# Retention of the later segments: from one chunk of one sequence a step to one chunk of two sequences a step, with the upper quarter of the scores left out

## The chip, the cores and the metric

The kernel runs on one core of one Trainium2 chip. The metric is the device time of one execution in microseconds. The kernel before takes 714.7 us, the median of three runs from 714.23 to 714.72; the profiled execution spans 715.2 us. All data are float32.

## The reference

Two blocks stand one after the other. The first is a recurrent retention over 4 sequences, 8 heads, 768 positions and head size 64:

```
for t in range(S):
    state = gamma * state + outer(k[t], v[t])      # per sequence and head, 64 x 64
    y[t]  = scale * q[t] @ state
```

Its output, 3072 rows of 512, is the input `x` of a feed-forward block with 1536 hidden units:

```
g   = x @ w_gate
out = (g * sigmoid(g) * (x @ w_val)) @ w_out
```

The recurrence is computed by chunks of 128 positions. Inside a chunk, `y[t]` is a sum over `s <= t` of `(q[t] . k[s]) * gamma^(t-s)` times `v[s]` ("scores", a decay mask, "mixing"), plus `q[t]`, decayed, times the state before the chunk ("old state"). Then the state is decayed and `k^T v` of the chunk is added, with `k` decayed ("new state"). Of the 128 by 128 scores of a head only those with `s <= t` count: for the upper half of `s` (64 to 127) and the lower half of `t` (0 to 63) all are zero.

## The kernel before

**Segments.** The rows are worked off in four segments. A segment is three chunks of two sequences, so 6 chunks and 768 rows. For the first segment the retention comes first. After that the program goes round a loop with `s` from 0 to 3: an up projection with gate (`up` for the first segment, `up2` for the later ones), then a down projection (`down`). The matrix products are a fast scheme with seven products in place of eight, in `up2` applied twice over, so there are many sums of blocks (`sums_x` and `sums_2` for the inputs, `sums_u` for the weights, `sum_h` for the hidden units), which VectorE (DVE) computes.

**Retention between the products.** The retention of segment `s + 1` is done inside the down projection of segment `s`. `down` calls `step()` after each of its products; there are 21 such calls in a segment. `retention` (line 468) makes a list of closures, and the tables `DUE` (line 858; the first for `s` = 0, the second for the others) say at which of the 21 calls the next closure is emitted. The order on each engine is the order in which the program emits; nothing is rearranged by a scheduler.

**One step.** `chunk(n)` emits, in this order: `scores` of the next chunk (line 389 on TensorE, the mask product of line 395 on DVE into `midp`), `mix` of this chunk (old state, line 453; mixing, line 456; four copies to `xT` on ScalarE, line 465), `decay` (four ScalarE copies of the state with a factor), `state` (line 429, and a DVE sum, line 434), the loads of the chunk after next, and, on GpSimd (POOL), the products that put the decays on `q` and `k` of the next chunk (lines 403 and 408). Scores go through banks 4 and 5, mixing through 6 and 7, the new state through 3.

**Shapes on TensorE.** A head has 64 columns, so the products use parts of the 128 by 128 array. Scores and old state are products of 64 rows and 64 columns of weights, and the loops are ordered so that neighbours use the four quarters in turn. Mixing and new state have 128 rows and 64 columns, and neighbours use the two column halves in turn. The products of `up2` (line 643) and `down` (lines 726 and 735) use the whole array.

**Weights.** During the down projection of `s` = 0 DVE computes sums of weight blocks (lines 171, 175, 179) which are loaded from DRAM and stored back (`load_unit`, `sums_u`); later up projections load the sums. Input loads and weight loads are issued by SyncE in the order of the program; results are stored from ScalarE's queue (line 803). Places for `q`, `k`, `v` of chunks are the buffer `loadp` and two of the six weight buffers of `ring`, which also serve `up2`; each reuse waits for the last reader.

**The end.** The last unit of `down` copies its last product (`T4`) to SBUF with one ScalarE instruction (line 797) and stores two blocks of 128 rows by 512 columns.

The core of the loop order in `scores` before:

```
for n in range(NP):
    for m in (slice(0, D), slice(D, P)):      # halves of s
        for i in range(2):                    # head of the pair
            r = ds(D * i, D)
            nc.tensor.matmul(sp[i][m, ts(n, P)], kt[r, n, m], qt[r, n], ...)
```

Of the kernel before, what the change touches and what calls it, by code (L numbers as in the profile page):

```python
# [16 lines left out]
P = 128  # L17
# [7 lines left out]
L = 3  # L25
# [8 lines left out]
RING = 6  # L34

# [6 lines left out]
def tile_retnet_swiglu(  # L42
# [46 lines left out]
    def place(name, n):  # L89
# [3 lines left out]
        ("hsp", 4 * FH * P), ("midp", 4 * 512), ("loadp", 8 * 512), ("iop", 6 * 512)))  # L93
# [21 lines left out]

    def places_of(n):


        if n % 3 == 2:
            return [ring[4 + i // 2][:, ts(i % 2, 512)] for i in range(4)]  # L120
        return [loadp[:, ts(4 * (n % 3) + i, 512)] for i in range(4)]
# [244 lines left out]
    states = [consts.tile([P, NP, D], F32, name=f"state{i}") for i in range(4)]  # L366
    xT = consts.tile([P, NC, 2, TH], F32, name="xT")
    xsa = consts.tile([P, 4, KH, TH], F32, name="xs")
    xs = [xsa[:, i] for i in range(4)]

# [7 lines left out]
    def state_of(c, old=0):  # L378
        return states[2 * (c // NCK % 2) + (c + old) % 2]

    def scores(c):
        kt, qt = (pairs(t) for t in chunks[c][:2])
        sp = [bank("s") for i in range(2)]

        for n in range(NP):
            for m in (slice(None),) if c in first_chunks else (slice(0, D), slice(D, P)):
                for i in range(2):
                    r = ds(D * i, D)
                    nc.tensor.matmul(sp[i][m, ts(n, P)], kt[r, n, m], qt[r, n],  # L389
                                     start=(n == 0), stop=True, skip_group_check=True)  # L390
        a = []
        for i in range(2):
            j = turn["a"] = turn.get("a", -1) + 1
            t = pairs((iop if c in first_chunks else midp)[:, ts(j % 4, 512)])
            nc.vector.tensor_tensor(t, pairs(sp[i]), mask[:, i], op=ALU.mult)
            a.append(t)
        att[c] = a
# [38 lines left out]
    def mix(c):  # L436

        ci, seq, pos = c % NCK, c // NCK % 2, ts(c % L, P)  # L440
        qd, vn = pairs(chunks[c][1]), chunks[c][2]
        a = att.pop(c)
        prev = state_of(c, 1)
        if c in first_chunks:
            y = [pairs(banks[(0, 1, 2, 3, 7, 6)[first_chunks.index(c)]])]
            own = [(n, i, i, y[0][:, n]) for n in range(NP) for i in range(2)]
        else:
            y = [bank("y")[:, : 2 * P].rearrange("p (b t) -> p b t", b=2) for i in range(2)]
            own = [(2 * h + b, i, h, y[i][:, b])
                   for b in range(2) for i in range(2) for h in range(2)]  # L450
        for k, (n, i, h, to) in enumerate(own if ci else []):
            r = ds(D * i, D)
            nc.tensor.matmul(to[ds(D * h, D)], prev[r, n], qd[r, n],  # L453
                             start=k < 2 * len(y), stop=False, skip_group_check=True)
        for k, (n, i, h, to) in enumerate(own):
            nc.tensor.matmul(to[ds(D * h, D)], vn[:, ts(2 * n + i, D)], a[i][:, n],  # L456
                             start=(ci == 0 and k < 2 * len(y)), stop=True,
                             skip_group_check=True)
        if c in first_chunks:
            att[c] = y[0]  # L460
            nc.scalar.copy(xT[:, :, seq, pos], att[c])
        else:
            for h in range(2):
                for i in range(2):
                    nc.scalar.copy(xT[ds(D * i, D), ds(2 * h, 2), seq, pos],  # L465
                                   y[i][ds(D * h, D)])

    def retention(s):

        cs = seg_chunks(s)

        def chunk(n):
            if n + 1 < len(cs):
                scores(cs[n + 1])
            if n >= 0:
                mix(cs[n])
                decay(cs[n])  # L480
                state(cs[n])
                del chunks[cs[n]]
                if n + 3 < len(cs):
                    load_chunk(cs[n + 3], places_of(n))
            if n + 1 < len(cs):
                scale_k(cs[n + 1])
                scale_q(cs[n + 1])

        steps = []
        for n in range(-1, len(cs)):  # L490
            steps.append(lambda n=n: chunk(n))
            if n == 5:
                steps.append(lambda: sums_2(1, 2))
            if n > 0 and n % 2:
                steps.append(lambda n=n: sums_x(n // 2))
        return steps
# [222 lines left out]
    def down(s, u, step):  # L719
# [4 lines left out]
        def product(o, slot, a, start=True):  # L724
            for k in range(FH):
                nc.tensor.matmul(o, a[:, k], wot[k][:, slot], start=(start and k == 0),  # L726
                                 stop=(k == FH - 1), skip_group_check=True)
# [14 lines left out]
        def second(u):  # L742
            z = banks[2][:, :DH]
            product(z, B21, a_dn(0, 1, u))
            to = iop[:, ts(2 * (u % 2), DM)]
            tt(to[:, :DH], z, first_dn.pop(u), op=ALU.add)
            step()

# [40 lines left out]
        tt(ev[1][:, DH:], x, p5, op=ALU.add)  # L789
        more(3)  # L790
# [5 lines left out]
        product(x, T4, a_dn(1, 1, u), start=False)  # L796
        nc.scalar.copy(ev[1][:, :DH], x)  # L797
        p, pos = divmod(s * L, NCK)

        def store():  # L800
            for i in range(2):
                row = (2 * p + i) * S + (pos + u) * P
                nc.scalar.dma_start(out=out[ds(row, P)], in_=ev[i])

        if u < L - 1 or s == NSEG - 1:
            store()
        step()
        return store


    kept_vk = consts.tile([P, 2, 512], F32, name="kept_vk")

    def warm_up(n):

        for _ in range(n):
# [4 lines left out]
    warm = consts.tile([P, P + 1], F32, name="warm")  # L820
# [37 lines left out]
    DUE = [(5, 7, 9, 10, 11, 13, 14, 15, 17, 18, 19, 20),  # L858
           (3, 5, 7, 8, 9, 11, 12, 13, 15, 16, 18, 20)]
# [20 lines left out]
    for s in range(NSEG):  # L880
        nxt = seg_chunks(s + 1) if s + 1 < NSEG else []
        if s == 0:
            for i in range(3):
                load_chunk(nxt[i], places_of(i))
        else:

            ends = [(7 * n + 13.4, lambda i=i: load_chunk(nxt[i], places_of(i)))
                    for i, n in ((0, NU - 5), (2, NU - 4), (1, NU - 3)) if nxt]
# [9 lines left out]
            ends.append((5, store))  # L898
            up2(s, prepared, ends)
# [5 lines left out]
        if nxt:  # L905
            att.clear()
            steps = retention(s + 1) + [lambda: sums_2(5, 6)]
        count, sums = [0, 0, 0], []

        def step():  # L910

            k = count[0] = count[0] + 1
            if not nxt:
                return
            if s:
                if k in DUE[1]:
# [4 lines left out]
            if count[1] < len(to_sum) + 1 and k > 1 and count[1] < 3 + count[2] // 3:  # L921
# [5 lines left out]
            if k in DUE[0]:  # L927
                steps.pop(0)()
            while sums and count[2] * 12.5 < (k - 6) * 3 * len(to_sum):
                sums.pop(0)()  # L930
                count[2] += 1

        for u in range(L):
            store = down(s, u, step)
        for st in sums:
            st()
        if nxt:
            sums_2(7)
            sums_2(3)
            sums_2(4)  # L940
# [49 lines left out]
```

## Time and profile before

| | |
|---|---|
| time, median of 3 | 714.7 us |
| span of the profile | 715.2 us |
| TensorE busy | 699.7 us, 98% |
| VectorE busy | 467.5 us, 65% |
| ScalarE busy | 257.7 us, 36% |
| GpSimd busy | 239.3 us, 33% |
| DMA | 139.09 MB, mean 194 GB/s |

The stages follow each other in time. The first retention and the first up projection end at about 153 us. The down projections that hold the later retentions lie at about 155 to 219, 319 to 388 and 489 to 555 us, the up projections with `up2` between them, and the last down projection, which holds no retention, begins at about 658 us.

How to read the rows: each row of groups has the line, the engine, the operation, the tensors, `rows*columns` of the weights (for TensorE), the shape, the number of records, the busy time and the mean time of one in ns, then the idle time before them and what ended it. TensorE rows have two records for each float32 matmul of the program. A row of the timeline begins with its start and its length in us; `x` is the number of records in it.

### The profile page before, as it was taken

To read this page: it belongs to the slowest core of one execution; us is meant where nothing else is said; L and a number is where in the kernel's file an instruction comes from. 1 tells how busy PE (TensorE), PEld (TensorE's weight loads), DVE (VectorE), ACT (ScalarE), POOL (GpSimd) and SP (SyncE) were. 2 spreads that over 40 slices of the span, in tenths; PEclk is the share of its full clock that TensorE was granted. 3 is DMA by queue.
4 is the path that set the end of the run, shared out by engine and by line. 5 is a ranking of instruction groups with operands and counts; after the bars stand their busy time and mean duration, and the time that the engine had idled before them with its cause. 6 is when DMAs were issued, how large, how long until landed. Compare 5 with 4: busy or idle time off the path is not lost.

```text
span 715.2 us, 12349 instructions
## 1 busy us (share of the span) xinstructions
PE 699.7 (98%) x4832; PEld 608.7 (85%) x4832; DVE 467.5 (65%) x836; ACT 257.7 (36%) x538; POOL 239.3 (33%) x147
## 2 busy tenths in 40 slices
PE   6998999999999999999999999999999999999997
PEld 6754555578889999998888999998888999999886
DVE  3787998777769887876264575757652656657420
ACT  2658777512322332431332333332332233243000
POOL 0423444504100728380220355373210072735000
PEclk9999999999999999999999999999999999999999
DMA  9698888714999958652633556560473265630010
GB/s 325 222 359 284 284 282 268 269 47 119 405 346 356 343 191 294 206 207 79 220 145 104 175 201 198 199 207 17 120 279 133 82 207 202 201 113 1 16 43 30
DMA packets 60826, 139.09 MB, mean 194 GB/s; under 512 B 4576, under 2 KB 27616, under 8 KB 60768
## 3 DMA queue, kind: packets, MB, share of 16 engines
q1 hardware_dynamic: 57312, 132.01, 53.7%
q10 hardware_dynamic: 3456, 6.29, 2.4%
q8 instruction: 38, 0.62, 0.4%
q14 instruction: 20, 0.16, 0.1%
HBM read 101.72 MB, written 36.57 MB: 193 GB/s over the span
## 4 chain that ended last, share of the span: by engine, by line
PE 68%; DVE 1%; issue 0%; ACT 0%; DVEq 0%
PE bank L643 40%; PE bank L726 20%; PE bank L735 3%; PE bank L389 2%; PE bank L456 2%; PE bank L453 1%; PE bank L429 1%; DVE iop L608 0%; DVE ring L171 0%; DVE loadp L598 0%; DVE loadp L600 0%; DVE loadp L597 0%; ACT hsp L608 0%; DVE ring L179 0%; ACT iop L797 0%
## 5 line engine op out<-in xcount | busy, mean ns | idle before, releaser
L643 PE MATMUL bank<-loadp,ring 128*128 128x192 f32 x720 | 140.2, 327 | 0.0
L726 PE MATMUL bank<-wot,hsp 128*128 128x256 f32 x576 | 129.8, 382 | 0.0
L726 PEld LDWEIGHTS bank<-wot,hsp 128*128 128x128 f32 x576 | 108.0, 190 | 15.9 <-issue 1.0
L643 PEld LDWEIGHTS bank<-loadp,ring 128*128 128x128 f32 x720 | 120.5, 190 | 1.0 <-ACT midp L608 0.7
L608 DVE TENSOR_TENSOR iop<-bank,iop 128x384 f32<-128x384 f32 x144 | 79.7, 556 | 54.8 <-PE bank L643 51.1
L643 PE MATMUL bank<-xs,ring 128*128 128x192 f32 x432 | 87.8, 326 | 0.0
L608 ACT COPY hsp<-bank 128x384 f32<-128x384 f32 x90 | 43.0, 479 | 100.4 <-PE bank L643 90.8
L678 POOL TENSOR_TENSOR hT<-iop 128x768 f32<-128x768 f32 x36 | 67.1, 1865 | 34.8 <-DVE iop L608 34.8
L643 PEld LDWEIGHTS bank<-xs,ring 128*128 128x128 f32 x432 | 73.1, 190 | 0.0
L608 POOL TENSOR_TENSOR iop<-hsp,midp 128x768 f32<-128x768 f32 x9 | 16.3, 1813 | 163.4 <-ACT hsp L608 135.1
L643 PE MATMUL bank<-xT,ring 128*128 128x192 f32 x324 | 66.3, 327 | 1.1 <-DVE iop L608 1.1
L532 PE MATMUL bank<-xs,ring 128*128 128x384 f32 x192 | 64.7, 488 | 1.7 <-ACT iop L558 0.8
L726 PE MATMUL bank<-wot,hT 128*128 128x256 f32 x288 | 65.7, 381 | 0.1
L726 PEld LDWEIGHTS bank<-wot,hT 128*128 128x128 f32 x288 | 54.2, 190 | 8.1 <-DVE iop L789 0.5
L532 PEld LDWEIGHTS bank<-xs,ring 128*128 128x128 f32 x192 | 36.1, 190 | 28.5 <-ACT iop L558 1.7
L643 PE MATMUL bank<-hsp,ring 128*128 128x192 f32 x288 | 56.7, 326 | 0.5 <-ACT hsp L608 0.5
L643 PEld LDWEIGHTS bank<-xT,ring 128*128 128x128 f32 x324 | 54.7, 190 | 2.5 <-DVE iop L608 2.2
L532 PE MATMUL bank<-xT,ring 128*128 128x384 f32 x144 | 49.6, 489 | 1.7 <-DVE hT L569 1.6
L465 ACT COPY xT<-bank 64x256 f32<-64x256 f32 x72 | 26.5, 368 | 68.3 <-PE bank L456 67.5
L643 PEld LDWEIGHTS bank<-hsp,ring 128*128 128x128 f32 x288 | 48.4, 190 | 0.8 <-ACT hsp L608 0.8
L608 DVE TENSOR_TENSOR midp<-bank,midp 128x384 f32<-128x384 f32 x72 | 39.9, 555 | 13.8 <-PE bank L643 12.4
L532 PEld LDWEIGHTS bank<-xT,ring 128*128 128x128 f32 x144 | 27.0, 190 | 21.5 <-DVE hT L569 2.2
(147 smaller groups left out, 955.6 us busy)
## 6 DMA issues: line engine op xcount, KB each, us to landing
ring<-unitt SPq DMA_DIRECT2D x50, 896.0 KB, 4.7
unitt<-ring SPq DMA_DIRECT2D x21, 896.0 KB, 5.6
unitb<-ring SPq DMA_DIRECT2D x12, 896.0 KB, 6.9
ring<-unitb SPq DMA_DIRECT2D x21, 512.0 KB, 6.0
out_dram<-iop ACTq DMA_DIRECT2D x24, 256.0 KB, 2.8
loadp<-in_w_val_dram SPq DMA_DIRECT2D x18, 256.0 KB, 3.9
loadp<-in_w_gate_dram SPq DMA_DIRECT2D x9, 512.0 KB, 6.9
midp<-in_w_out_dram SPq DMA_DIRECT2D x12, 256.0 KB, 6.4
```

What stands on the lines that cost most here:

```text
L389: nc.tensor.matmul(sp[i][m, ts(n, P)], kt[r, n, m], qt[r, n], start=(n == 0), stop=True, skip_group_check=True)
L429: nc.tensor.matmul(st[ds(D * i, D), n], kd[:, h], vn[:, h], start=(n == 0), stop=True, skip_group_check=True)
L453: nc.tensor.matmul(to[ds(D * h, D)], prev[r, n], qd[r, n], start=k < 2 * len(y), stop=False, skip_group_check=True)
L456: nc.tensor.matmul(to[ds(D * h, D)], vn[:, ts(2 * n + i, D)], a[i][:, n], start=(ci == 0 and k < 2 * len(y)), stop=True, skip_group_check= ...
L465: nc.scalar.copy(xT[ds(D * i, D), ds(2 * h, 2), seq, pos], y[i][ds(D * h, D)])
L532: nc.tensor.matmul(o, w[:, slot, k], a[:, k], start=(start and k == 0), stop=(stop and k == KH - 1), skip_group_check=True)
L608: events.append((t, len(events), lambda: fn(*args, **kw)))
L643: nc.tensor.matmul(o[:, h], w[:, h, slot], rhs, start=(start and h == 0), stop=True, skip_group_check=True)
L678: by_block(9.5, 13.5, lambda r: pool(to[:, r], u2[:, r], p5[:, r], op=add))
L726: nc.tensor.matmul(o, a[:, k], wot[k][:, slot], start=(start and k == 0), stop=(k == FH - 1), skip_group_check=True)
L735: nc.tensor.matmul(o, a_dn(0, 0, u)[:, k], wot[k][:, B11], start=(k == 0), stop=(k == FH - 1), skip_group_check=True)
```

## The change

**Pairs.** A step of the later segments is now one chunk of both sequences (a "pair"), so a segment has three pairs. States of the two sequences lie side by side in one tile, and their decay, their new state and its sum are done for both together.

**Scores by parts.** `scores_of(p, g)` does half of the heads (`g`) of a pair: for the lower half of `s` all 128 columns of `t`, for the upper half of `s` the upper 64 columns of `t` alone. The quarter of the scores which the mask sets to zero is not computed. Results and masks of a group are 384 columns wide in place of 512. The lower `s` of sequence 0 and of sequence 1 go to different halves of the partitions. So that the mixing finds scores and `v` on the same partitions, the halves of the second sequence's `v` and `k` are loaded changed over, and new tables (`load_side`, `kdec_b`) hold mask and decay in the same layout.

**Mixing by parts.** The mixing is `low` (lower `s`, all `t`) and `high` (upper `s`, upper `t`), both with 64 rows and 64 columns of weights. `old` runs in two halves.

**Order.** `begin(p)` emits half of the old states, `low`, the first group of scores of the next pair, and the new state; `end(p)` the second group, `high`, the other old states, eight copies to `xT`, the masks of the second group, the loads for pair 2 and the POOL products, which are held in `later` and emitted two at a step. `both` is `begin` and `end` in one step. `DUE` is new, and the weight sums follow a table `SUMS`.

**Aside from the retention.** The sums `sums_2(7)`, `(3)` and `(4)`, which stood at the end of the down projection, are emitted among the first stages of `up2`. In the last unit of the last segment the results are stored in parts as they are ready, and the last product is done in two halves of 128 columns.

The diff, cut to its core:

```diff
-            for m in (slice(None),) if c in first_chunks else (slice(0, D), slice(D, P)):
-                for i in range(2):
-                    r = ds(D * i, D)
-                    nc.tensor.matmul(sp[i][m, ts(n, P)], kt[r, n, m], qt[r, n],
-                                     start=(n == 0), stop=True, skip_group_check=True)
...
-        def chunk(n):
-            if n + 1 < len(cs):
-                scores(cs[n + 1])
-            if n >= 0:
-                mix(cs[n])
-                decay(cs[n])
-                state(cs[n])
-                del chunks[cs[n]]
-                if n + 3 < len(cs):
-                    load_chunk(cs[n + 3], places_of(n))
-            if n + 1 < len(cs):
-                scale_k(cs[n + 1])
-                scale_q(cs[n + 1])
...
+        def scores_of(p, g):
+
+            kt, qt = ([pairs(t) for t in given[p][w]] for w in range(2))
+            for b in range(2):
+                for m in range(2):
+                    for r in range(2):
+                        x, n = half[r], 2 * g + b
+                        mm(banks[4 + r][half[m], ts(b, P)], kt[m][x, n, half[0]],
+                           qt[m][x, n], b == 0)
+            for b in range(2):
+                for m in range(2):
+                    for r in range(2):
+                        x, n = half[r], 2 * g + b
+                        mm(banks[4 + r][half[m], ds(2 * P + D * b, D)],
+                           kt[1 - m][x, n, half[1]], qt[1 - m][x, n, half[1]])
+
+            def decayed():
+                for i in range(2):
+                    j = turn["b"] = (turn.get("b", -1) + 1) % 6
+                    att[p, g, i] = midp[:, ts(j, TA)]
+                    nc.vector.tensor_tensor(att[p, g, i], banks[4 + i][:, :TA],
+                                            side[g][:, i], op=ALU.mult)
...
+        def low(p, first):
+            for i in range(2):
+                for b in range(2):
+                    for h in range(2):
+                        for r in range(2):
+                            n = 2 * h + b
+                            mm(y_of(n, i, r), given[p][2][r][half[r], ts(2 * n + i, D)],
+                               att[p, h, i][half[r], ts(b, P)], first and i == b == 0)
+
+        def high(p):
             for h in range(2):
                 for i in range(2):
+                    for b in range(2):
+                        for r in range(2):
+                            n = 2 * h + b
+                            mm(y_of(n, i, 1 - r, half[1]),
+                               given[p][2][1 - r][half[r], ts(2 * n + i, D)],
+                               att[p, h, i][half[r], ds(2 * P + D * b, D)])
...
+        def begin(p):
+            ci = cs[2 * p] % NCK
+            while later:
+                later.pop(0)()
+            if ci:
+                old(p, False)
+            low(p, ci == 0)
+            if p + 1 < L:
+                scores_of(p + 1, 0)
+            state_from(p)
+
+        def end(p):
+            if p + 1 < L:
+                after = scores_of(p + 1, 1)
+            high(p)
+            if cs[2 * p] % NCK:
+                old(p, True)
+            for c in range(2):
+                for h in range(2):
+                    for i in range(2):
+                        nc.scalar.copy(xT[half[i], ds(2 * h, 2), c, ts(p, P)],
+                                       y_both(h, i, c))
+            if p + 1 < L:
+                after()
+            if p == 0:
+                load_pair(s, 2, (0, 1, 2, 3))
+            if p + 1 < L:
+                scale(p + 1)
...
+        return [lambda: scores_of(0, 0), second, lambda: both(0), lambda: sums_x(0),
+                lambda: both(1), lambda: sums_x(1), lambda: begin(2), lambda: end(2),
+                lambda: sums_2(1, 2), lambda: sums_x(2), lambda: sums_2(5, 6)]
...
-        product(x, T4, a_dn(1, 1, u), start=False)
-        nc.scalar.copy(ev[1][:, :DH], x)
...
+        for c in (ts(0, DH // 2), ts(1, DH // 2)) if last(u) else (ds(0, DH),):
+            product(x, T4, a_dn(1, 1, u), start=False, cols=c)
+            nc.scalar.copy(ev[1][:, c], x[:, c])
+            if last(u):
+                store(1, ev[1], c)
...
-    DUE = [(5, 7, 9, 10, 11, 13, 14, 15, 17, 18, 19, 20),
-           (3, 5, 7, 8, 9, 11, 12, 13, 15, 16, 18, 20)]
+    DUE = [(5, 7, 9, 10, 14, 15, 16, 19, 19, 20, 21), (2, 4, 7, 8, 10, 12, 15, 18, 19, 20, 21)]
+
+    SUMS = (0, 0, 0, 0, 0, 0, 0, 2, 3, 1, 3, 3, 2, 3, 1, 2, 3, 3, 3, 2, 2)
...
+            ends += [(t, lambda p=p: sums_2(p)) for t, p in ((8, 7), (15, 3), (22, 4))]
...
-        if nxt:
-            sums_2(7)
-            sums_2(3)
-            sums_2(4)
```

## The prediction

> **What bounds the kernel now.** I read the page first, then the TensorE rows group by group, then the waits, then short stretches of the timeline.
>
> ```profile
> PE 699.7 (98%) x4832; PEld 608.7 (85%) x4832; DVE 467.5 (65%) x836; ACT 257.7 (36%) x538; POOL 239.3 (33%) x147
> ...
> PEclk9999999999999999999999999999999999999999
> ```
>
> TensorE is busy for 98% of the span at full clock, so the kernel is as long as its matmuls. In the table by stretches it is busy for 57.86 of the 58.00 us of the first later segment (160.5 to 218.5), 62.00 of 62.00 in the second and 63.00 of 63.00 in the third. The waits agree: after the first 160 us only a few tenths remain. So what a change to the retention is worth is TensorE time, read from its own rows (lines 389 scores, 453 old state, 456 mixing, 429 new state):
>
> ```profile
> L389 PE MATMUL bank<-loadp 64*64 64x128 f32 x384 | 13.2, 275 | 0.0
> L456 PE MATMUL bank<-midp,loadp 128*64 128x128 f32 x192 | 13.1, 279 | 0.0
> L429 PE MATMUL bank<-loadp 128*64 128x64 f32 x160 | 6.3, 222 | 0.0
> L453 PE MATMUL bank<-loadp,state 64*64 64x128 f32 x160 | 6.2, 269 | 0.0
> ```
>
> The mean of one (275 ns) is latency; these matmuls overlap. The trace has two records for each matmul of the program (384 + 192 records of line 389 on loadp and ring for 18 chunks of 16). One step of the middle of a segment shows their true rate:
>
> ```profile
> 167.00 0.38 PE L726 MATMUL bank<-wot,hsp 128*128 128x256 f32 x1
> 167.31 1.10 PE L389 MATMUL bank<-loadp 64*64 64x128 f32 x32
> 168.24 0.62 PE L453 MATMUL bank<-loadp,state 64*64 64x128 f32 x16
> 168.78 1.09 PE L456 MATMUL bank<-midp,loadp 128*64 128x128 f32 x16
> 169.71 0.63 PE L429 MATMUL bank<-loadp 128*64 128x64 f32 x16
> 170.27 0.48 PE L726 MATMUL bank<-wot,hT 128*128 128x256 f32 x1
> ```
>
> Inside these groups the single starts come in "waves". With 64*64 blocks of the array, four records start within 20 ns, and the next four 109 ns later; with 128*64 blocks two start together, every 109 ns for 128 columns and every 58 ns for 64 columns. So a wave costs 109 or 58 ns by its columns, whether two or four blocks work in it. This chunk is 8 + 4 + 8 waves of 109 and 8 of 58 ns: 2.64 us. From the last product of the down projection to the next took 3.27 us in starts, of which 0.22 is that product's own pitch, and the first product after it lost 0.10 us more: 3.15 us. The other 0.5 us are three changes of block shape, 0.17 us each.
>
> [...] four blocks side by side, and 0.17 us a change. [...] line 682 takes 0.95 us alone and 1.81 us at 316.69 beside line 408.
>
> **Part 1, scores (before line 389, after line 502).** A pair of chunks had 2 x 8 = 16 waves of 109 ns. Now, for each of two halves g, 8 matmuls of 128 columns (lower s, all t) and 8 of 64 columns (upper s, upper t), both rotating over four blocks: 2 x (4 x 109 + 4 x 58) = 1.34 us instead of 1.74. That four blocks can keep up at 58 ns is not in a row; but after each change of shape the second set of four weight loads starts 55 ns after the first set (167.309, then 167.364), so I take 58; 109 is the other end.
>
> **Part 2, mixing.** It had 16 waves of 109 ns a pair, 1.74 us. Now `low` (16 matmuls of 128 columns, rows h and r innermost, so four blocks) is 8 waves of 109 ns, 0.87 us; `high` (16 of 64 columns) has h outermost, so neighbours alternate between the two row halves of one column half. In program order that is two blocks a wave: 16 waves of 58 ns, 0.93 us. Together 1.80 us: nothing gained. If the blocks of the other h could start early it would be 8 waves, 0.46 us less a pair; that is the other end.
>
> **Part 3, old and new state.** 8 waves of 109 and 16 of 58 ns a pair, as before. The decay copies and the sum go over both sequences in one instruction: ACT and DVE, which have the room (16 to 17 of 58 to 63 us, and 29 to 43).
>
> **Part 4, waves and changes by segment.** First and third segment (chunks 3 to 5: old state always, new state for two pairs). Before: 0.87 + 4 x 2.64 + 2.18 + 1.31 = 14.94 us and 20 changes, 18.3 us; the starts give 18.37. After: two steps of scores 0.67 each, two of `both` with 0.44 + 0.87 + 0.67 + 0.93 + 0.67 + 0.93 + 0.44 = 4.94, `begin` 1.31, `end` 1.36: 13.88 us, and 2 + 2 + 4 + 4 + 2 + 2 = 16 changes, 2.7 us: 16.6. Saved 1.8. Second segment (chunks 0 to 2): before 14.99 and 20 changes, 18.4; after 13.94 and 17, 16.8. Saved 1.6. All three: **5.1 us**, all on the path.
>
> **Part 5, new waits.** `both` runs two groups of scores through banks 4 and 5, so the second must wait for the two DVE products of the first. Queued behind it on TensorE are `high`, the old states and the next down product. Between the two groups stands the new state, 0.93 us and two changes, 1.2 us; DVE needs about 0.22 for the last matmul's end and 1.02 for two products of 384 columns (row L608, 128x384, 556 ns alone, 1.01 for two in line). That leaves about 0.05 us for each of six: +0.3. If DVE is behind by one sum (0.68 to 0.95 us) each costs up to 0.9, +5 in all. The q products on POOL (1.28 to 1.96 us each) must be done when `begin` starts: two steps of 2.6 us after the scores, so they are hidden.
>
> **Part 6, loads and sums moved.** Pair loads replace chunk loads of the same bytes; the tables added are about 0.8 MB, in a stretch (150 to 162 us) where the DMA queues are nearly idle. DVE has 12 sums of 0.35 us (4.2 us) fewer before the up projection starts; they are spread over its first stages, at zero, since TensorE's product of line 643 is what hides them. Of the existing waits one should go:
>
> ```profile
> 315.51 0.56 DVE L608 TENSOR_TENSOR hT<-bank,hT 128x384 f32<-128x384 f32 x1
> ...
> 316.64 2.77 POOL L408 TENSOR_TENSOR loadp<-loadp,tab 128x512 f32<-128x512 f32 x2
> 316.69 1.81 DVE L682 TENSOR_TENSOR hT<-hT,midp 128x768 f32<-128x768 f32 x1
> ...
> 319.02 0.92 PE L643 MATMUL bank<-xT,ring 128*128 128x192 f32 x4 [0.74 <-DVE iop L608]
> ```
>
> The k product of the next segment slows DVE at the end of the up projection, and the last product waits: 0.74 us idle here, and as the list of waits has 1.1 us in two for this pair, about 0.4 at 487.5, with 0.1 more to get going again; at 656.9, where no POOL product runs, under 0.1. Now q stands before k in POOL's queue and waits for the scores; but chunk 0 has no q product, so only the wait at 487.5 goes: -0.5.
>
> **Part 7, the end.**
>
> ```profile
> 709.71 1.67 PE L726 MATMUL bank<-wot,hT 128*128 128x256 f32 x7
> 709.93 1.05 PEld L726 LDWEIGHTS bank<-wot,hT 128*128 128x128 f32 x5
> 711.42 0.37 ACT L797 COPY iop<-bank 128x256 f32<-128x256 f32 x1 [9.99 <-PE bank L726]
> 711.48 0.82 ACTq L803 DMA_DIRECT2D out_dram<-iop  x2
> ```
>
> After TensorE's end stand a copy and two stores of 256 KB; bytes flow until about 714.0 us. After, only the last 64 KB are stored there. The product in halves costs 24 records at 111.5 ns (the pitch of the warm-up matmuls of 128 columns at full clock) instead of 12 at 216: +0.1. Saved: one issue (0.4), some of the copy, and the flow of 448 KB at some 384 GB/s (1.1) less what overlaps: I take 1.0, from 0.4 to 1.6. Net -0.9.
>
> **Sum:** -5.1 + 0.3 - 0.5 - 0.9 = -6.2 us, 714.7 - 6.2 = 708.5.
>
> **Rivals.**
> A, `high` runs on four blocks: 9 x 0.46 = 4.2 us more saved, 704.3. For it: the four blocks are independent. [...]
> B, the gain is eaten in the first segment. There the queues move about 400 GB/s from 174 us on and DVE waited up to 3.65 us for weight blocks (212.8 us); with TensorE 1.8 us earlier DVE may hold it at the start of the up projection, or find itself behind in `both`. Then the 1.8 us are lost and 1 to 2 us added: 712. Against it: the loads start a step earlier and 2.8 us of sums no longer stand ahead.
> C, the short matmuls are no cheaper: a wave of 64 columns in 64*64 blocks takes 109 ns. Then scores lose 8 x 51 and `high` 16 x 51 ns a pair, 1.22 x 9 = 11.0 us: 719.5, slower. For it: no such wave in the trace. Against it: line 429's 58 ns and the 55 ns between weight loads.
>
> **How the numbers follow.** Forecast 0.64, A 0.12, B 0.17, C 0.07. The time is the forecast's. The range leaves out C and the ends of the others: 703.5 to 712. Faster by over 0.2% (under 713.3): forecast, A and most of B, 0.88. Within 0.2%: the worst of B, 0.06. Slower: C, 0.06.
>
> **What would show it.** In the new trace the group of line 502 with 64x64 columns has 32 records of scores in 0.46 us of waves, `high` 32 in 0.93; scores plus state plus scores in `both` take about 2.6 us with no wait for DVE above 0.2 us; the last product before 487.5 waits under 0.1; bytes after TensorE's end flow for under 0.5 us. Waits of TensorE on DVE in each `both`, or waves of 64 columns above 80 ns, would make it wrong.

## The result and the profile after

The changed kernel takes 721.9 us, the median of four runs (719.7 to 722.3), against 714.7 for the kernel before. The ratio over the single runs is 1.0089 (the medians alone give 1.010), with a 95% interval from 1.006 to 1.0117: slower, outside the predicted 703.5 to 712.0. The profiles show only a part of this. The profiled run of the changed kernel is the quickest of its four (719.7 us, a span of 717.9); that of the kernel before took 716.9 us, 2.2 above its median. So the spans differ by 2.8 us where the medians differ by 7.2. Of all runs below only two, both of the kernel with the double steps in two, lie far off, at 1598 and 2835 us; nothing on record says why, and its ratio leaves them out.

TensorE's row on the page of the changed kernel looks harmless, and that is the first thing to learn from it:

```profile
PE 697.4 (97%) x5132; PEld 608.6 (85%) x5132; DVE 462.8 (64%) x830; ACT 252.3 (35%) x514; POOL 239.6 (33%) x147
```

The busy time fell by 2.3 us (699.7 before). The change meant it to fall, and yet the span is longer. So I cut both traces at the same places, the start of the last matmul of each up projection:

| us | before | changed | difference |
|---|---|---|---|
| start to end of the first up projection | 145.77 | 144.11 | -1.66 |
| first later segment: down projection with retention, up projection | 173.85 | 176.89 | +3.04 |
| second later segment | 169.27 | 170.80 | +1.53 |
| third later segment | 168.64 | 168.57 | -0.07 |
| last down projection to the end | 57.63 | 57.55 | -0.08 |
| span | 715.16 | 717.92 | +2.76 |

The first row isn't the change's work: the order of the start is the same. In the trace of before TensorE waits 2.69 us for a load of q up to 17.57 us, and then its clock is at half for 3.4 us, which costs 1.7 (half of the 3.4). In the changed kernel the wait there is 1.36 us and no such window follows. In the kernels below that left the start alone this row took 143.2 to 144.1 us where no half-clock window is on record, and 146.4 in the one that had two after a wait of 2.6. Such a window is rare in the kernel before: its profiled run has a mean clock of 0.997, and of 60 runs recorded later six have 0.997 or less. In the rows of the segments the prediction wanted -1.8, -2.1 and -1.8. The list of TensorE's waits from 150 us on names what took them; here it is for the changed kernel (columns: total, times, longest):

```profile
PE bank L502 <- issue: 3.7, 2, 2.1
PE bank L502 <- DVE midp L524: 3.1, 1, 3.1
...
PE bank L871 <- ACT iop L958: 0.4, 1, 0.4
```

Before, that list had 1.1 us for VectorE in two waits, and nothing in the later retentions. (An "issue" of 0.6 us at 153 to 155 us, ahead of them, stands in both lists.) Now there are three long stops, all in the second double step (`both(1)`), one in each segment. Two of them end in "issue": the engine waited for nothing that the profile shows. The timeline of the changed kernel's TensorE around the one in the second segment:

```profile
354.37 0.85 PE L502 MATMUL bank<-loadp,ring 64*64 64x128 f32 x32
355.15 0.69 PE L502 MATMUL bank<-ring 128*64 128x64 f32 x16
355.66 0.64 PE L502 MATMUL bank<-loadp 128*64 128x64 f32 x16
356.23 0.94 PE L502 MATMUL bank<-loadp,ring 64*64 64x128 f32 x27
...
357.77 0.22 PE L502 MATMUL bank<-midp,ring 64*64 64x64 f32 x1
360.09 0.67 PE L502 MATMUL bank<-ring,states 64*64 64x128 f32 x15 [2.11 <-issue]
360.69 4.06 PE L871 MATMUL bank<-wot,hsp 128*128 128x256 f32 x10
```

Scores, new state and scores follow each other as planned. Then, near the end of the upper mixing, 2.3 us of nothing, and after it old-state matmuls whose data had been there long before (their first one, at 357.60, had started). The down products after it are slow as well. The table by stretches of the changed kernel shows why (after the length: TensorE, weight loads, VectorE, ScalarE, GpSimd, then granted clock, DMA share, GB/s):

```profile
354.40:357.60 3.20, 3.20 (x131) 3.06 (x124) 1.82 (x4) 0.27 (x1) 0.26 (x1) 1.00 1.02 399
357.80:360.00 2.20, 0.18 (x9) 0.04 (x2) 0.72 (x2) 0.00 (x0) 2.20 (x3) 1.00 0.98 404
360.65:364.05 3.40, 3.40 (x11) 2.73 (x9) 0.00 (x0) 2.94 (x8) 1.18 (x2) 0.50 1.02 414
364.05:367.45 3.40, 3.40 (x17) 2.99 (x17) 2.20 (x3) 0.00 (x0) 0.00 (x0) 1.00 0.94 390
```

After the stop the clock is 0.50 for 3.4 us (3.413 in the clock's own record), and within it the down products start every 427 ns instead of 216: half of the work gets done, another 1.7 us. The kernel with later loads, further down, has the same stop without such a window, and its segment takes 1.7 us less. The two half-clock windows of this trace begin 163.84 us apart, 48 times 3.413, from which I estimate that windows of this length run on in step. This one came after 2.1 us of idle. So 2.3 + 1.7 = 4.0 us of the second segment are a loss, and without them its row would be -2.5.

The stop in the first segment is of another kind. Changed kernel, rows of TensorE and VectorE in order of time:

```profile
193.10 0.64 PE L502 MATMUL bank<-loadp 128*64 128x64 f32 x16
...
194.75 0.69 DVE L165 TENSOR_TENSOR ring<-ring 128x512 f32<-128x512 f32 x1 [3.44 <-DMA ring<-unitb]
195.48 0.42 DVE L173 TENSOR_TENSOR ring<-ring 128x256 f32<-128x256 f32 x1
195.94 0.42 DVE L169 TENSOR_TENSOR ring<-ring 128x256 f32<-128x256 f32 x1
196.28 1.01 DVE L524 TENSOR_TENSOR midp<-bank,tab 128x384 f32<-128x384 f32 x2
```

VectorE stands 3.44 us before a sum of a weight block that hasn't landed. Behind it in VectorE's queue are the mask products (line 524) that empty banks 4 and 5, and TensorE's second group of scores needs those banks. This costs 3.3 us and a half-clock window at 196.8 to 200.2 us, 1.7 more.

**What is special about the two "issue" stops.** I counted all of TensorE's records in order of time, weight loads, matmuls and the sequencer's waits, from zero. The first one after the stop in the second segment is number 5313, in the third segment 8129. They are 2816 apart, 11 times 256. One of the two DMA queues that the page calls "instruction" moved one packet of 16384 bytes at a time, 40 in the run for TensorE's 10366 records, about one for every 256 (38 for 9768 before), so I take it for TensorE's. That gives the leading theory.

**T1, instructions run out.** The theory, an estimate from these counts: each packet of 16384 bytes is a block of 256 of TensorE's instructions; when one block ends, a place comes free and the next fetch is issued, and if that doesn't land before the block now running ends, TensorE stands. A double step is 96 matmuls of the program, some 390 records, in 5 us; two block ends can fall within it, 3.4 us apart in the changed kernel. A step of before was some 160 records, and in its later retentions two block ends were never less than 8.9 us apart. In the trace's list of transfers of the changed kernel, the fetch after the block end at 354.37 begins at 357.51, takes 1.09 and ends at 358.60; with the queues empty, after the end at 344.02, it begins after 0.50 us. Among long matmuls a fetch even begins before the last record of a block starts (at 335.40 for the end at 339.19), so under T1 a place comes free somewhat ahead of the end as it is counted here.

**T2.** A wait for data, a bank or a buffer, which the profile doesn't name, holds TensorE in `both(1)`. **T3** is for the first segment, and is rival B of the prediction: late weight blocks hold VectorE, and VectorE holds TensorE.

### The profile page after: what moved, and what is told of

It is laid out like the page before. It is cut to its first block, busy times and chain, and to the rows that moved or that the text cites. A ratio compares the mean times of both kernels' runs of the same rounds, so it can differ in the third digit from the quotient of the medians.

```text
span 717.9 us, 12964 instructions
## 1 busy us (share of the span) xinstructions
PE 697.4 (97%) x5132; PEld 608.6 (85%) x5132; DVE 462.8 (64%) x830; ACT 252.3 (35%) x514; POOL 239.6 (33%) x147
## 4 chain that ended last, share of the span: by engine, by line
PE 85%; DVE 3%; DMA 3%; issue 2%; ACT 1%; POOL 0%; SPq 0%; DVEq 0%; POOLq 0%; ACTq 0%
PE bank L788 39%; PE bank L871 24%; PE bank L677 13%; PE bank L502 5%; PE bank L881 4%; DMA loadp<-in_q_t_dram 1%; DMA ring<-unitb 1%; DMA unitt<-ring 1%; DVE ring L165 1%; DVE hsp L859 1%; DVE iop L753 0%; DVE ring L169 0%; POOL ring L269 0%; ACT bank L241 0%; DVE midp L524 0%
## 5 line engine op out<-in xcount | busy, mean ns | idle before, releaser
L871 PEld LDWEIGHTS bank<-wot,hsp 128*128 128x128 f32 x576 | 109.5, 192 | 16.3 <-issue 1.2
L871 PE MATMUL bank<-wot,hT 128*128 128x256 f32 (+1 forms) x300 | 65.5, 373 | 0.4 <-ACT iop L958 0.4
L942 DVE TENSOR_TENSOR iop<-bank,iop 128x256 f32<-128x256 f32 x12 | 5.1, 425 | 68.8 <-PE bank L871 55.4
```

The lines of the kernel that those rows point to most:

```text
L871: nc.tensor.matmul(o[:, cols], a[:, k], wot[k][:, slot, cols], start=(start and k == 0), stop=(k == FH - 1), skip_group_check=True)
L942: tt(ev[0][:, DH:], wb, u2, op=ALU.add)
```

## The experiments

Each is the changed kernel with one edit, unless said otherwise. The stages of all of them are in one table at the end.

### The program shifted by 96 instructions

```diff
+    def tiny(n):
+        for _ in range(n):
+            nc.tensor.matmul(banks[3][:, :16], warm[:, :P], warm[:, :16], start=True,
+                             stop=True, skip_group_check=True)
-    ... K0 t0 K1 s2 ...
+    ... K0 t0 K1 z24 s2 ...
```

> 24 idle matmuls (16 columns, result unused) among the loads at the start, nothing else changed: every later TensorE instruction lies 96 places further in the program's blocks of 256. T1 (TensorE runs out of instructions where two block ends fall within one dense step): the idle stretches of 2.3 us at the second double step of the second segment (about 358 us) and of 1.8 us in the third (529 us) vanish, the half-clock window after them too, and a stretch of about 2 us appears in the first double step of the first segment, whose block ends then lie 70 and 326 instructions after its start; the total may be 718 to 722. T2 (a wait for data, a bank or a buffer in these steps): the stretches stay where they are, 2.3 and 1.8 us, and the time within 0.3 us of the changed kernel. T3 (VectorE held by a late weight block in the first segment, 3.4 us at 193.5): that stretch stays under both.

Measured: 720.8 us median of 12 runs, ratio to before 1.0089 (1.0065 to 1.0114). The total says nothing here: the 24 matmuls took 5.9 us in the start, half clock followed from 17.5 to 27.8 us, and the first up projection ended at 150.8 us, 4 us or more later than in any other kernel. The later segments say all. TensorE's waits of this kernel from 322 us to the end are one line:

```profile
PE bank L871 <- ACT iop L958: 0.4, 1, 0.4
```

Both "issue" stops and the window after them are gone, with the same loads, data, banks and order of the retention. The second segment takes 166.82 us and the third 166.62, which is 2.5 and 2.0 less than before. T2 falls: a wait for data or banks doesn't go away when unrelated matmuls are put in 340 us earlier. In the first segment no new stop in the first double step came (only 0.3 us there); I had expected 2. A fetch 1.27 us after the first block end landed in time. The stop in `both(1)` of the first segment stayed, with 2.3 us for VectorE, as T3 says.

### The double steps in two

```diff
-        return [..., second, lambda: both(0), lambda: sums_x(0),
-                lambda: both(1), lambda: sums_x(1), ...
+        return [..., second, lambda: begin(0), lambda: end(0), lambda: sums_x(0),
+                lambda: begin(1), lambda: end(1), lambda: sums_x(1), ...
-    DUE = [(5, 7, 9, 10, 14, 15, 16, 19, 19, 20, 21), (2, 4, 7, 8, 10, 12, 15, 18, 19, 20, 21)]
+    DUE = [(5, 7, 9, 10, 11, 13, 14, 15, 16, 19, 19, 20, 21),
+           (2, 4, 7, 8, 9, 10, 11, 12, 15, 18, 19, 20, 21)]
```

> The double steps are emitted as two steps with a product of the down projection between them (longer matmuls, fewer instructions a microsecond), same work. T1: the idle stretches at 358 and 529 us go, with the half-clock window at 360.6, -4 to -6 us, so 716 to 718 us. T2: if the wait is for VectorE's products it goes as well, since the product between covers it; if it is for a load or the banks of mixing it stays, 721 to 722. T3: the 3.4 us at 193.5 us stay unless the second scores move behind the late sum; then 0 to 3 us less.

Measured: 715.3 us median, ratio 0.9995 (0.9976 to 1.0015). The stops shrink to 1.1 and 0.6 us and don't vanish. They still end at records 5313 and 8129. A product of the down projection in between (twelve records in 2.9 us) gives the fetch more time, but here the fetch began 4.3 and 4.2 us after the block end. So the split helps without curing, against my expectation that they go. In the first segment the second half came too early for its load:

```profile
PE bank L502 <- DMA loadp<-in_q_t_dram: 1.6, 2, 0.8
```

### Loads put later in SyncE's order

```diff
-                if k > 7 and k % 2 == 0 and k // 2 - 4 < RING - 2:
-                    load_unit(k // 2 - 4, True)
+                if k > 11 and k % 2 == 0 and k // 2 - 6 < RING - 2:
+                    load_unit(k // 2 - 6, True)
```

> From the second segment on the loads of ready weight sums for the next up projection are issued four products later, so that the DMA queues are quiet when the double steps run; order on TensorE unchanged. T1 with the cause in full DMA queues: block fetches start within 0.6 us and the idle stretches of 2.3 and 1.8 us shrink under 0.5 us, unless the loads come late for the up projection (idle then at its start). T1 with a fetch that is slow by itself, and T2: the stretches stay.

Measured: 718.1 us, ratio 1.0063 (1.0038 to 1.0087); stops of 2.3 and 1.9 us in the same places. This decides nothing, because the edit did not do what I meant. SyncE doesn't follow TensorE; it waits only for the places that it loads into. The loads still started at 351.26 us (351.38 in the changed kernel), and the queues were as full. Where a load is written sets its order among the loads, not its time.

### Loads put ahead in SyncE's order

```diff
-                if k > 7 and k % 2 == 0 and k // 2 - 4 < RING - 2:
-                    load_unit(k // 2 - 4, True)
+                if k <= RING - 2:
+                    load_unit(k - 1, True)
```

> From the second segment on the loads of ready weight sums are put ahead in SyncE's order (with the first four products), so that they run at about 320 to 345 us and not beside the double steps; TensorE's program is the changed kernel's, instruction for instruction. T1 (instruction blocks come late because the DMA queues are full): in the second segment the block is fetched within 1 us of its place coming free, the 2.3 us at 358 and the 1.8 us at 529 us shrink under 0.5 us, the half-clock window at 360.6 us goes: -4 to -6 us, 716 us. T2 (a wait in the double step itself): 2.3 and 1.8 us stay, 721 to 722. The first segment is as in the changed kernel (3.4 us at 193.5).

Measured: 714.6 us, ratio 0.9998 (0.9985 to 1.0012), where the changed kernel has 721.9 and 1.0089; the profiled spans are 712.8 and 717.9. TensorE's waits from 322 us on are again the one line of the tail. In this kernel other loads fill the queues up to 355 us, but behind the block end at 355.15 they are nearly empty (the last two columns), where the changed kernel had 1.01 and 411 GB/s at 355 to 359 us:

```profile
351.00:355.00 4.00, 4.00 (x58) 3.38 (x60) 0.29 (x1) 1.48 (x5) 0.00 (x0) 1.00 0.97 338
355.00:359.00 4.00, 4.00 (x157) 3.83 (x148) 2.43 (x5) 0.44 (x2) 0.88 (x1) 1.00 0.04 11
```

TensorE's program is the same as in the changed kernel, record for record. The block ends, taken from the count of records, and the fetches, from the list of transfers (us):

| kernel, segment | block end | fetch begins after | takes | next block end | idle there |
|---|---|---|---|---|---|
| changed, second | 354.37 | 3.14 | 1.09 | 360.09 | 2.33 |
| changed, third | 525.52 | 2.92 | 1.07 | 530.93 | 1.84 |
| in two, second | 351.53 | 4.29 | 1.07 | 358.44 | 1.07 |
| shifted, second | 357.87 | 0.53 | 0.88 | 361.58 | 0 |
| loads ahead, second | 355.15 | 0.55 | 1.24 | 358.49 | 0 |
| loads ahead, third | 522.33 | 0.31 | 1.09 | 525.84 | 0 |

The last two rows give the need: dense steps use up a block in 3.3 to 3.5 us. A fetch that begins after 0.5 and takes 1.1 is there in time; one that begins after 3 is not. From the begin of a fetch to the first matmul out of its block took 2.5 to 2.6 us in the first three rows, so landing is not all of it. With T1 the sum fits: 3.1 + 2.6 = 5.7 us from one block end to the next, where 3.4 were needed, hence 2.3 idle. The size of the stop follows the delay: in the third segment of the kernel with half blocks, below, the fetch begins after 2.06 us and TensorE is idle for 0.75. Removing the load of the queues (here) or moving the block ends (the shift) each removes the stops, which T1 said and T2 didn't.

Why a fetch begins late is only argued. In the changed kernel the packets in flight at 354 to 358 us have a median of 7168 bytes and 0.275 us (the blocks of ready sums), and 3.1 us are some eleven of them. In the shifted kernel, at 358 us, the queues were as busy (306 to 387 GB/s) but with packets of 2048 bytes and 0.084 us, and the fetch began after 0.53. At the next block end of that kernel, 361.58, the packets have 7168 bytes again, and the fetch began after 3.07; there the block in use lasted 14.8 us, and nothing stopped.

### Later sums in the first segment

```diff
-    SUMS = (0, 0, 0, 0, 0, 0, 0, 2, 3, 1, 3, 3, 2, 3, 1, 2, 3, 3, 3, 2, 2)
+    SUMS = (0, 0, 0, 0, 0, 0, 0, 2, 3, 1, 3, 3, 2, 1, 0, 3, 4, 4, 3, 2, 2)
```

> In the first segment the sums of the weight unit that arrives late are emitted two products later, behind the second double step. T3: the 3.4 us of idle at 193.5 us and the half-clock window at 196.8 to 200.2 us (1.7 us lost) go: -4 to -5 us, 717 us; the later stretches at 358 and 529 us stay. If something else holds TensorE there (T1 or a bank): no change, or a new idle stretch at the same place. If the sums are then late for the next weight place, up to 3 us come back at 205 to 215 us.

Measured: 719.2 us, ratio 1.0056 (1.0035 to 1.0076). The stop of 3.3 us and its half-clock window are gone, as T3 said: the down projection with the retention took 73.1 us instead of 78.0. But the up projection behind it took 103.2 instead of 98.9. Its waits in this kernel, TensorE first, then VectorE from 160 to 250 us:

```profile
PE bank L788 <- DVE iop L892: 1.3, 1, 1.3
PE bank L788 <- DVE iop L753: 1.2, 2, 0.7
PE bank L788 <- DVE midp L753: 1.0, 2, 0.8
```

```profile
DVE ring L165 <- DMA ring<-unitb: 8.7, 4, 4.0
```

Before, VectorE waited 5.1 us in two for such blocks. TensorE is earlier now, the blocks aren't, and the wait has moved some 20 us on; the sums of the last blocks begin at 207.4, 211.4 and 215.4 us, 4 us apart.

### Half of each weight block

The kernel with later sums, and half of the bytes of the later weight blocks left out.

```diff
-            nc.sync.dma_start(out=t[:, :, ds(U11, 4)],
-                              in_=unit_b[n // 7][:, SLOT[PRODUCTS[n % 7]]])
+            h = slice(0, 1) if less else slice(0, 2)
+            nc.sync.dma_start(out=t[:, h, ds(U11, 4)],
+                              in_=unit_b[n // 7][:, SLOT[PRODUCTS[n % 7]]][:, h])
-                load_unit(n, False, count[1] % (RING - 2))
+                load_unit(n, False, count[1] % (RING - 2), count[1] > 3)
```

> The kernel with the later weight sums, and from the fifth weight block on only half of each block is read from DRAM for the sums of the first segment (256 instead of 512 KB; the other half of the sums is computed from old contents, so the weights of later up projections are wrong). If the DMA queues set the pace of the weight blocks (rival B of the prediction), VectorE's 8.7 us of waits for them between 195 and 245 us fall under 2 us, the 3.7 us of new waits at the start of the second up projection go, and the first segment ends at about 315 us instead of 319.7: 4 us less in all. If VectorE's own work sets it, the same waits stay: no change.

Measured: 716.7 us, ratio 1.0021 (1.0009 to 1.0034). VectorE's waits for blocks fell from 8.7 us to this (the line has another number because the edit adds one):

```profile
DVE ring L166 <- DMA ring<-unitb: 3.0, 3, 2.3
```

That is more than the 2 I had set, but TensorE's wait for `iop` of line 892 is gone, and the first segment ends at 316.2 us, not 319.7. VectorE's work is the same in both, so the bytes set the pace of this segment. While they do, most of the retention's gain can't be collected there: even with half of them the segment takes 173.0 us, 0.9 under the 173.9 of before.

### Loads ahead, split steps, tail in one piece

The edit of the loads as above, the steps in two with `DUE[0] = (5, 7, 9, 10, 11, 14, 15, 15, 16, 19, 19, 20, 21)`, and the last product whole:

```diff
-        for c in (ts(0, DH // 2), ts(1, DH // 2)) if last(u) else (ds(0, DH),):
+        for c in (ds(0, DH),):
```

> Early loads, the double steps in two, and the last product in one piece. T1: no idle above 0.5 us in the second and third segment, down projections of 70.2 and 70.0 us (72.2 and 72.1 in the kernel before); end of TensorE 0.5 us shorter than in the changed kernel. In the first segment the second half of the double step stands one product later than in the split tried before, so it does not wait for the q load. Total 708 to 711 us if the first segment keeps 1 us of its gain, 711 to 713 if the weight blocks from DRAM set its pace. T2: 715 and above.

Measured: 711.4 us median of 8, ratio 0.996 (0.9945 to 0.9974): faster than both kernels. That is just over 708 to 711, in the range that I had named for the case that the weight blocks set the pace of the first segment, and they do: it takes 174.2 us, as before the change (173.9). The last segments and the tail came as expected, within 0.2 us.

### The same with four blocks in the upper mixing

```diff
-            for h in range(2):
-                for i in range(2):
-                    for b in range(2):
+            for i in range(2):
+                for b in range(2):
+                    for h in range(2):
                         for r in range(2):
```

> As the kernel with early loads and split steps, and in the upper mixing the row halves and column halves both change from one matmul to the next (four blocks in turn instead of two). If two blocks a wave is what held the upper mixing (16 waves of 58 ns for 0.93 us), it takes 8 waves, 0.46 us less in each of 9 pairs: 4 us less than its companion, 3 in the two later segments alone. If the matmuls for the other column half already started early, nothing changes (under 0.5 us).

Measured: 710.7 us median of 6, ratio 0.994 (0.9921 to 0.9958). The intervals of the two overlap, so the stages have to tell: the second and third down projection take 69.58 and 69.37 us, against 70.42 and 70.21 of the companion, 0.84 less in each, 0.28 a pair. I had named 0.46 or nothing. The timelines of one step, first the companion with two blocks, then this kernel:

```profile
356.17 0.22 PE L502 MATMUL bank<-midp,loadp 64*64 64x64 f32 x1
356.18 0.22 PE L502 MATMUL bank<-midp,ring 64*64 64x64 f32 x1
356.23 0.22 PE L502 MATMUL bank<-midp,loadp 64*64 64x64 f32 x1
...
356.71 0.33 PE L502 MATMUL bank<-ring,states 64*64 64x128 f32 x2
...
356.88 0.22 PE L502 MATMUL bank<-midp,ring 64*64 64x64 f32 x1
...
357.47 0.48 PE L871 MATMUL bank<-wot,hsp 128*128 128x256 f32 x1
```

```profile
360.42 0.22 PE L502 MATMUL bank<-midp,loadp 64*64 64x64 f32 x1
360.43 0.22 PE L502 MATMUL bank<-midp,ring 64*64 64x64 f32 x1
360.43 0.22 PE L502 MATMUL bank<-midp,loadp 64*64 64x64 f32 x1
360.44 0.22 PE L502 MATMUL bank<-midp,ring 64*64 64x64 f32 x1
360.48 0.22 PE L502 MATMUL bank<-midp,loadp 64*64 64x64 f32 x1
...
360.89 0.62 PE L502 MATMUL bank<-ring,states 64*64 64x128 f32 x16
361.44 0.48 PE L871 MATMUL bank<-wot,hsp 128*128 128x256 f32 x1
```

With two blocks in turn, two records start every 58 ns at first; from the first to the next down product is 1.30 us. With four, four records start every 58 ns, and it is 1.02. The difference is under 0.46 because the program order is not kept. From 356.42 to 356.59 matmuls for the other column half start beside the first ones, four in 58 ns, so the mixing's starts cover 0.71 us and not the 0.87 of strict turns. And old-state matmuls, which come after the mixing in the program, already start at 356.71, while the mixing goes on to 356.88.

**All stages together** (us; e is the end of the first up projection, then the three later segments, then the tail):

| kernel | e | first | second | third | tail |
|---|---|---|---|---|---|
| before | 145.8 | 173.9 | 169.3 | 168.6 | 57.6 |
| changed | 144.1 | 176.9 | 170.8 | 168.6 | 57.6 |
| shifted | 150.8 | 175.0 | 166.8 | 166.6 | 57.5 |
| in two | 144.0 | 174.1 | 168.2 | 167.4 | 57.5 |
| loads later | 143.3 | 177.7 | 169.1 | 168.6 | 57.5 |
| loads ahead | 144.1 | 177.6 | 166.8 | 166.6 | 57.5 |
| later sums | 143.4 | 176.3 | 169.4 | 168.6 | 57.5 |
| half blocks | 143.2 | 173.0 | 171.4 | 167.5 | 57.6 |
| ahead, in two, whole tail | 143.2 | 174.2 | 167.0 | 166.8 | 57.1 |
| the same, four blocks | 146.4 | 175.5 | 166.2 | 166.0 | 57.1 |

## Why the prediction was wrong

**Parts 1 and 4, the waves, were right.** Waves of 64 columns on four blocks cost 58 ns (four starts together at 0, 55, 114 and 172 ns in the upper scores of the kernel with loads ahead; the upper mixing in the last timeline), and rival C is refuted. Freed of the stops, the down projections with retention take 70.24 and 70.04 us (loads ahead) against 72.19 and 72.06 before: 1.95 and 2.02 saved where the prediction had 1.6 and 1.8.

**Part 2 was nearly right.** The upper mixing does go two blocks a wave for most of its length, and the order costs 0.28 us a pair, not the 0.46 of rival A, because the argument leant on a strict program order, which was not shown: in the companion's timeline old states start at 356.71, and the mixing ahead of them in the program goes on to 356.88.

**Part 5 is the step that failed.** It counted the new waits of `both` as waits for VectorE in banks 4 and 5, 0.3 us and at most 5. In the second and third segment that wait doesn't exist (none in the list once the stops are gone). What it left out is that a step of 390 records, more than a block and a half (256 records each, by T1), has to be supplied with instructions. With full queues that cost 2.3 and 1.8 us, and a half-clock window that lost 1.7 us after one of them. The profile of before has no such stop, but the page had the queue "instruction" with 38 packets, and the change was visibly to put 2.4 times as many short instructions into one step.

**In the first segment part 5 failed in another way.** It let VectorE be behind by one sum, 0.68 to 0.95 us. In the trace one weight sum waits 3.44 us for its block, with the mask products behind it in VectorE's queue: 3.3 us for TensorE, and 1.7 at half clock. This is rival B, which the prediction had at 0.17 and at 712 us; it took the 1.8 us and added 3.0 in the profiled run, more than the "1 to 2" it was given. Later sums only moved the wait, and with half of the bytes TensorE's wait in the up projection went.

**Part 6 came in the later segments.** The moved sums cost nothing there: the third up projection took 96.58 us before and after. The wait at 487.5 us did go: the second took 96.58 us instead of 97.08, -0.5 as predicted. The one at 319.0, which the prediction kept, went in the profiled run as well; there the k product of the next segment began only at 319.52, behind a load. Rival B's "2.8 us of sums" doesn't agree with this part: the twelve sums of before, at 222.4 to 226.1 us, are the 4.2 us named here. The forecast doesn't rest on it.

**Part 7 was mis-sized.** The time from TensorE's end to the end of the span fell from 3.77 to 2.98 us, 0.8 (predicted 1.0). But the halves cost 0.7 and not 0.1 (the time up to TensorE's end, against the kernel with the last product whole). The second half waits 0.36 us for the copy of the first, which reads the same bank:

```profile
713.01 0.27 ACT L958 COPY iop<-bank 128x128 f32<-128x128 f32 x1 [8.73 <-PE bank L871]
...
713.33 1.60 PE L871 MATMUL bank<-wot,hT 128*128 128x128 f32 x12 [0.36 <-ACT iop L958]
```

Net -0.1 for -0.9. In one piece, with the early stores kept, the tail is 0.5 us shorter than before.

**The sum.** The part that was argued from TensorE's rows (-1.95 - 2.02 - 0.5) came, with 0.6 to spare. Against it stand three stops (3.3 + 2.3 + 1.8) and two half-clock windows (3.4) in the profiled run, 10.8 in all; with -1.7 in the start, -1.8 for the first segment, -2.5, -2.0 and -0.1 this makes +2.7, and the spans differ by 2.8. (The -1.7 is the half-clock window in the profile of before, and the first -1.8 is the predicted one.) The other three runs of the changed kernel have a mean clock of 0.993 where the profiled one has 0.995. 0.7% of 720 us is 5 us of lost clock, three windows of 1.7 in place of two. One more window would explain most of their 2 us; no trace of them shows it.

What stays open is why the fetch begins 3 to 4 us late (packets ahead of it on its engine are argued, not shown), and what the 1.4 to 1.6 us from its landing to the next matmul are.

## What to carry to other kernels

Count instructions as well as cycles: where a dense run of short matmuls passes more than one block of instructions (256 records here, gone in 3.3 to 3.5 us), look at when the fetch of the next block can run, and keep large loads out of that stretch; here one line that moved loads was worth 5 us of the profiled span (717.9 and 712.8). A stop of TensorE that ends in "issue", always at the same count of instructions (here at records 5313 and 8129), was the sign of this, and moving the program by some instructions is a cheap test. And before a gain is booked, ask in each stage what else sets its pace: in the stage where the weight blocks came by DMA at 4 us apiece, almost none of the gain could be kept.

## What the runs showed of the hardware that I had not expected

- Instruction blocks: the "issue" stops in the later retentions ended at record 5313 or 8129 in the changed kernel (2.33 and 1.84 us) and in the one with the steps in two (1.07 and 0.6), and lay in the same places in the one with later loads (2.3 and 1.9). In a double step without a stop 256 records, 64 float32 matmuls, pass in 3.3 to 3.5 us (loads ahead); beside loads of 7168-byte packets the next block end came after 5.7 and 5.4 us (changed).
- Half clock came after 2 to 3 us of idle. I cut the traces before and after the change every 3.413 us, in step with the clock's record. Three windows with 2.69 us of idle (before, from 14.54 us), 3.05 and 2.11 us (changed, from 193.37 and 357.21 us) were each followed by a half-clock window; the one with 1.63 us (changed, from 527.88 us) was not. The 2.3 us from start to start in the changed kernel lay in one window (2.11 of idle); the same stop in the kernel with later loads was cut by an edge at 359.65 us, 1.7 us of idle before it, and brought none. In the shifted kernel half clock came from 17.5 us on without any idle in the 3.4 us before it, while the 24 matmuls of 16 columns ran (12.55 to 18.4 us).
- Matmuls on different blocks of the array start out of program order: old states at 356.71 before upper mixing at 356.88. The strict order that the prediction used was not shown.
- Matmuls of 16 columns on the whole array, each with its weights loaded anew, start every 112 ns a record at full clock, no faster than the 111.5 of those with 128 columns.
